# Values as scaled float16 pairs, two product passes, and one DMA transpose per half of p

## The chip, the cores and the metric

The kernel runs on one core of a Trainium2 chip. Five engines matter: PE multiplies matrices, DVE, ACT and POOL work on vectors, and SP issues DMAs from one queue in program order. Each engine takes its instructions strictly in the order in which the program holds them; semaphores make one wait for another. The metric is the device time of one execution in microseconds (us), lower is better.

## The reference

Eight batches of eight heads of attention with 576 tokens and head size 64, masked by blocks of 64, followed by a two-layer network on all 4608 tokens. Everything is float32.

```python
scores = (1 / np.sqrt(64)) * np.matmul(q, k.transpose(0, 1, 3, 2))
scores = np.where(pos[:, None] // 64 >= pos[None, :] // 64, scores, -1e9)
scores = scores - np.max(scores, axis=-1, keepdims=True)
attn = np.exp(scores)
attn = attn / (np.sum(attn, axis=-1, keepdims=True) + 1e-09)
x = np.matmul(attn, v)             # then (B, H, S, D) -> (B*S, H*D) = (4608, 512)
h = x @ w_in                       # (512, 2048)
out = np.maximum(0.01 * h, h) @ w_out   # (2048, 512)
```

## The kernel before

**Order of the work.** The body of the kernel does not run instructions, it records them. `add(choices, rank, reads, writes, ...)` stores one operation with the engines that could do it, a rank and the keys of the buffers that it reads and writes. `Plan.run` then plays the program with a small table of costs (for SP, `TISSUE` and `TTILE` say what it believes the issue of a DMA transpose to cost) and writes out a fixed order for each engine: whichever operation is ready in that play and has the lowest rank goes next. The constants `RL`, `RV`, `RX`, `RN`, `LEAD`, `LAG` and so on shift the ranks, in units of one head. On the chip the order is fixed; only the waits are real.

**Heads.** `attention(i)` records one head. The eight heads of the first batch are done in two parts ("lo", "hi") by plain float32 products while the weights of the network are loaded and split. The other 56 heads (8 to 63, kind "full") are what the change is about. Such a head has its scores on PE, its maxima on DVE, exponentials on ACT (tiles `prow` or `slab`, five tiles t = 0 to 4 of up to 128 query rows), and its row sums in `sums`, inverted into `rec`.

**p in halves.** `parting(t)` multiplies the exponentials by `rec` into a float16 high half `part(0)`, and takes the float16 rest as low half `part(1)`. The tile holds both halves interleaved in blocks of 128 columns. `turn` issues one DMA transpose per tile on SP that moves both halves into `turned[y2]`: five per head, of 2, 4, 6, 8 and 10 blocks. `turned` has two buffers, y2 = 0 and 1, used by every other head. So a head's first transpose waits for PE to have finished the product of the head two before.

**v in three terms.** The values come by one DMA per head; `vs` keeps them as three bfloat16 terms v0, v1, v2 (two copies and two subtractions on ACT, DVE or POOL). In the product, `inner(j, y, w)` multiplies the weights [v0|v1] with both halves of p and the weights [v2|0] with the high half: three passes over 512, 448, 320 and 192 columns. `outer(w)` does the pieces for the first and the last 64 tokens as two products of 256 and 128 columns into another PSUM bank, whose partial sums DVE adds up by a `tensor_reduce` over three column groups (L760) and two additions (L769). `put_x` adds the upper 64 rows of the PSUM tile to the lower ones (L256/L255, L715) and stores x.

**The network.** `scale_x` takes the sum of squares of finished tokens on ACT and a scale from it; `split_x` makes float16 pairs of x; `ffn1` and `ffn2` are the two layers in chunks of 256 tokens, three passes each, with their results in `p_h` and `p_o`. They are recorded with ranks between the heads' and fill PE between the heads. When attention is over the rest of them remains.

**SP's queue** holds, per full head, the load of q and k (L495), the load of v (L505), five transposes (L633), and now and then stores of the output (L897).

Of the kernel before, what the change touches and what calls it, by code (L numbers as in the profile page):

```python
# [35 lines left out]
DB0 = 16  # L36

RL = 2.512
RP = 0.116
RB = 0.594  # L40
RT = 2.547
RV = 2.777
RX = -0.691
RN = -0.668

LEAD = 3.0
LAG = 1.993
RS = 2.157
RG = -0.11
OFF1 = 4.036  # L50
OFF2 = -1.346
SL1 = 11.386
AHEAD = -0.758

LAT = 1550
HOLD = 262.256
# [182 lines left out]
def attention_ffn(ctx: ExitStack, tc: tile.TileContext, qk0: bass.AP, qk: bass.AP, v: bass.AP, w_in: bass.AP, w_out: bass.AP, out: bass.AP):  # L239
# [62 lines left out]
    vs = fixed([P, NT, 2, 2 * D], BF16, "vs", 2)  # L302
# [3 lines left out]
    for y in range(2):  # L306
        nc.gpsimd.memset(sums[y], 1.0)
        nc.gpsimd.memset(nm[y], 0.0)
        nc.gpsimd.memset(vs[y][:, :, 1, D : 2 * D], 0.0)
    xr = [fixed([P, ND, S], F32, "xr0"), None]  # L310
    raws = fixed([P, 2 * WIDE], I32, "raw", RAWS)
# [4 lines left out]
    diag = fixed([P, P], F32, "diag")  # L316
    both = fixed([P, 1], F32, "both")
    p_s = fixed([P, 2, 512], F32, "p_s", pool=psum)
# [11 lines left out]
    ob = [fixed([P, DM], F32, "ob"), None]  # L330

# [15 lines left out]
    parts = [[carve(y, [t + 1, 2, P], F16) for t in range(NT)] for y in range(2)]  # L347
    v_stage = [carve(y, [NT, D], F32) for y in range(2)]
# [14 lines left out]
    def weight_piece(num, rank, f, out_side):  # L363
# [98 lines left out]
    def attention(i):  # L462
# [38 lines left out]
        if plain_v:  # L501
            vt, vkey = lambda: vf[z][:, :nv], ("vf", z)
        else:
            vt, vkey = lambda: v_stage[y2][:, :nv], ("vt", y2)
        add([("SP", 475, lambda: nc.sync.dma_start(vt(), v[b, h, :, :nv]))], r0 - RL + VD, [], [vkey], lag=1.5 * dma(nv * P * D * 4))  # L505
# [14 lines left out]
        if not plain_v:  # L520
            v0, v1, v2 = vs[z][:, :, 0, 0:D], vs[z][:, :, 0, D : 2 * D], vs[z][:, :, 1, 0:D]
# [86 lines left out]
        def parting(t):  # L608
            n, c = qn[t], pc[t]
            by = rec[z][:n, t : t + 1]  # L610

            def p():
                x = rows_[t][:n, c:]
                return x if t == 0 else x.rearrange("p (j k) -> p j k", k=P)

            def part(y):
                x = parts[y2][t][:n]
                return x[:, 0, y, c:] if t == 0 else x[:, :, y, :]

            w = pw[t] - c  # L620
            add([
                ("POOL", pool1(w), lambda: nc.gpsimd.tensor_scalar(part(0), p(), by, 1.0, op0=ALU.mult, op1=ALU.mult)),
                ("ACT", act(w, True), lambda: nc.scalar.mul(part(0), p(), by)),  # L623
                ("DVE+", dve(w, True), lambda: nc.vector.tensor_scalar_mul(part(0), p(), by)),
            ], r0 - RN, [("rec", z, t)] + pkeys(t), [("ph", y2, t)])
            add([
                ("DVE+", dve(w), lambda: nc.vector.scalar_tensor_tensor(part(1), p(), by, part(0), op0=ALU.mult, op1=ALU.subtract)),  # L627
            ], r0 - RN, [("rec", z, t), ("ph", y2, t)] + pkeys(t), [("pl", y2, t)])

            def turn():  # L630
                src = parts[y2][t][:n].rearrange("p j y k -> p (j y k)")
                dst = turned[y2][:, 8:10, 2, BLK:P] if t == 0 else turned[y2][:, 0 : 2 * t + 2, t - 1, :]
                nc.sync.dma_start_transpose(dst, src)  # L633
# [59 lines left out]
        ptd = [("ptf", g[0]) for g in tgroups[kind]] if plain_v else [("pt", y2, t) for t in range(NT)]  # L693
# [14 lines left out]
        def put_x(x, c, t0, t1):  # L708
            n, dst, keys = t1 - t0, place(t0, t1), keys_of(t0, t1)
            if plain_v:  # L710
                add(copying(n, dst, lambda: p_t[x][0:64, c : c + n], sb=False), rx, [("t", x)], keys)
                return
            add(copying(n, dst, lambda: p_t[x][64:128, c : c + n], sb=False), rx, [("t", x)], keys)
            add(
                [("DVE", dve(n), lambda: nc.vector.tensor_add(dst(), p_t[x][0:64, c : c + n], dst()))],  # L715
# [23 lines left out]
        def inner(j, y, w):  # L739
            c = 128 * j - 64 if j else 0  # L740
            start, stop = j == 0 and y == 0 and w == 0, j == 3 and w == 1

            def go():
                src = turned[y2][:, 2 * j + y].rearrange("p t k -> p (t k)")[:, c:512]
                nc.tensor.matmul(p_t[x1][:, c:512], vs[z][:, j + 1, w, :], src, start=start, stop=stop)  # L745
# [3 lines left out]
        def outer(w):  # L749
            def go():  # L750
                src = turned[y2][:, 8 : 10 - w, 2:4, BLK:P]
                dst = p_t[x0][:, 2 * w * P : (2 + w) * P].rearrange("p (c a b) -> p c a b", a=2, b=BLK)
                nc.tensor.matmul(dst, vs[z][:, 0, w, :], src, start=True, stop=True)

            return RATEH * (2 - w) * P, go, LOADH
# [3 lines left out]
        add(  # L759
            [("DVE", dve(6 * BLK), lambda: nc.vector.tensor_reduce(  # L760
                p_t[x0][:, 6 * BLK : 8 * BLK], p_t[x0][:, : 6 * BLK].rearrange("p (c k) -> p k c", c=3), axis=AX.X, op=ALU.add
            ))], rx, [], [("t", x0)],
        )
        put_x(x0, 6 * BLK, 0, 64)
        put_x(x1, 0, *tokens[kind])
        late = place(512, 576)
        for r in (0, 64):
            add(
                [("DVE", dve(64), lambda r=r: nc.vector.tensor_add(late(), p_t[x0][r : r + 64, 7 * BLK : 8 * BLK], late()))],  # L769
                rx, [("t", x0)], keys_of(512, 576),  # L770
            )
# [34 lines left out]

    def regions(c0, c1):
# [8 lines left out]
    def scale_x(e, c0, c1, rank):  # L816
        spans_ = list(regions(c0, c1))
        for k, (_, b, o, ln, keys) in enumerate(spans_):

            def square(k=k, b=b, o=o, ln=ln):  # L820
                nc.scalar.activation(
                    junk[:, :, :ln], xr[b % 2][:, :, o : o + ln], AF.Square, accum_out=xn[:, 2 * e + k : 2 * e + k + 1]
                )

            add([("ACT", act(4 * ln, True) + 190, square)], rank, keys, [("xn", e, k), "junk"])
        x = bank()
        num = len(spans_)

        def total(k):
            nc.tensor.matmul(p_t[x][:, 0:1], ones, xn[:, 2 * e + k : 2 * e + k + 1], start=k == 0, stop=k == num - 1)  # L830
# [90 lines left out]
    for i in range(len(work) + 1):  # L921
        if i == 2 * H:

            def second(y):
                nc.gpsimd.memset(parts[y][0], 0.0)
                if y:
                    clear(prow[1])

            for y in range(2):
                new = [("ph", y, 0), ("vt", y)] + [(a, y, t) for t in range(NT) for a in ("ph", "pl", "pt")]  # L930
                new += [("p", 1, t) for t in range(NT)] + [(a, 1, d) for a in ("xh", "xl") for d in range(0, CH, BLK)] if y else [("x", 1, h, k) for h in range(H) for k in (0, 1)] + [("ob", 1)]
                kind = "wo" if y else "wi"
                add([("POOL", 1500 if y else 200, lambda y=y: second(y))], 0, [("val", bool(y), f) for f in range(NF)], new)
        if i in events:
# [5 lines left out]
            for k in range(num):  # L940
# [5 lines left out]
                ffn2(c, e, u, rank + (nxt - i) * LAG / num + 0.003)  # L946
        if i < len(work):
# [42 lines left out]
```

## Time and profile before

| | |
|---|---|
| median of 3 runs | 1123.3 us (1120.63 to 1124.39) |
| the profiled execution's own time | 1120.48 us |
| its span in the trace | 1118.7 us |
| busy: PE, DVE, ACT, POOL | 1070.5, 747.9, 670.8, 322.8 us |
| granted PE clock over the span | 0.988 |
| DMA transposes | 280, 3.2 us from issue to landing (median) |

The profile comes from one execution; times inside it count from the span's start. The execution's time is 1.8 us longer than the span. SP has no busy row of its own on the page, since issuing DMAs is not counted as busy; its instructions stand in the timeline as "SPq". A row of the timeline merges instructions of one kind that follow each other: start, length of the whole stretch, what, and how many (x10). In the view of a line, "min/median/max" are the lengths of single instructions.

### The profile page before, as it was taken

The numbers are of one execution on the slowest core, as the hardware profiler recorded it, in microseconds if no ns is written. First come the engines' busy times: TensorE is split into PE (matmuls) and PEld (weight loads), VectorE is DVE, ScalarE is ACT, GpSimd is POOL, SyncE is SP. The second block draws the span as 40 slices with busy tenths as digits, with TensorE's granted clock in tenths as the row PEclk, the third lists the DMA queues.
The fourth block names the chain that finished last, engine by engine and source line by source line (L and its number), as shares of the span: only waits on it lengthen the run. The fifth ranks groups of instructions, "written<-read, shape, count | busy, mean of one in ns | idle before, by whom it ended". The sixth has DMA issues, their size and how long they took to land.

```text
span 1118.7 us, 20505 instructions
## 1 busy us (share of the span) xinstructions
PE 1070.5 (96%) x7298; PEld 745.8 (67%) x7298; DVE 747.9 (67%) x1814; ACT 670.8 (60%) x1650; POOL 322.8 (29%) x339
## 2 busy tenths in 40 slices
PE   9999899858999999999999999999999999999998
PEld 7887566535666666666666666666667666666665
DVE  6888978888877877786766667787777777220000
ACT  6797767657666666664455656666666666332222
POOL 2114324434433233323232223322333232111221
PEclk9999999978999999999999999999999999999999
DMA  7747247675755556564636355665555544100000
GB/s 260 248 145 262 81 97 174 132 170 123 165 140 122 128 123 142 123 123 106 116 83 117 80 127 121 141 129 105 122 141 138 114 101 93 27 20 1 20 19 19
DMA packets 247461, 131.37 MB, mean 117 GB/s; under 512 B 220224, under 2 KB 229440, under 8 KB 247360
## 3 DMA queue, kind: packets, MB, share of 16 engines
q1 hardware_dynamic: 247360, 130.07, 49.2%
q8 instruction: 57, 0.93, 0.3%
q14 instruction: 44, 0.36, 0.1%
HBM read 67.37 MB, written 9.44 MB: 69 GB/s over the span
## 4 chain that ended last, share of the span: by engine, by line
PE 37%; DVE 25%; ACT 6%; issue 4%; DVEq 0%; ACTq 0%
PE p_o L885 16%; PE p_h L867 16%; DVE nm L564 6%; DVE slab L627 5%; PE p_t L745 3%; PE p_s L544 2%; ACT prow L581 2%; DVE qs L514 2%; ACT slab L581 1%; DVE p_t L760 1%; ACT slab L623 1%; DVE slab L265 1%; DVE vs L265 1%; DVE slab L715 1%; DVE kk L256 1%
## 5 line engine op out<-in xcount | busy, mean ns | idle before, releaser
L266 POOL TENSOR_TENSOR gl<-g,gh 128x512 bf16<-128x512 f32 x121 | 144.2, 1192 | 475.8 <-ACT gh L255 431.4
L867 PEld LDWEIGHTS <-wih 128*128 128x128 f16 x2304 | 224.2, 98 | 77.2 <-issue 1.1
L867 PE MATMUL p_h<-slab,wih 128*128 128x256 f16 x1152 | 196.8, 273 | 0.0
L564 DVE TENSOR_REDUCE nm<-p_s 128x1 f32<-128x320 f32 (+4 forms) x308 | 143.6, 489 | 44.8 <-ACT prow L581 23.1
L885 PE MATMUL p_o<-woh,gh 128*128 128x512 f16 x576 | 172.6, 381 | 0.0
L885 PE MATMUL p_o<-wol,gh 128*128 128x512 f16 x576 | 172.3, 381 | 0.0
L885 PE MATMUL p_o<-woh,gl 128*128 128x512 f16 x576 | 172.3, 381 | 0.0
L872 ACT ACTIVATE g<-p_h 128x512 f32<-128x512 f32 x144 | 85.2, 592 | 139.5 <-PE p_h L867 139.2
L885 PEld LDWEIGHTS <-gh 128*128 128x128 f16 x1152 | 108.2, 99 | 82.9 <-issue 1.2
L867 PE MATMUL p_h<-slab,wil 128*128 128x256 f16 x576 | 157.2, 273 | 0.0
L867 PE MATMUL p_h<-xh,wih 128*128 128x256 f16 x576 | 157.1, 273 | 0.0
L867 PE MATMUL p_h<-xl,wih 128*128 128x256 f16 x576 | 157.0, 273 | 0.0
L867 PE MATMUL p_h<-xh,wil 128*128 128x256 f16 x576 | 157.0, 273 | 0.0
L544 PE MATMUL p_s<-kk,qs 128*128 128x288 f32 (+2 forms) x592 | 122.8, 334 | 33.6 <-ACT prow L581 22.3
L581 ACT ACTIVATE prow<-p_s,nm 128x320 f32<-128x320 f32 (+4 forms) x168 | 88.9, 531 | 87.0 <-DVE nm L564 82.9
L581 ACT ACTIVATE slab<-p_s,nm 128x448 f32<-128x448 f32 (+4 forms) x140 | 73.2, 524 | 88.7 <-DVE nm L564 87.9
L867 PEld LDWEIGHTS <-wil 128*128 128x128 f16 x1152 | 112.8, 98 | 13.2
L544 PEld LDWEIGHTS p_s<-kk,qs 128*128 128x128 f32 x592 | 91.1, 193 | 44.7 <-ACT prow L581 26.6
L745 PE MATMUL p_t<-slab,vs 128*128 128x512 f16 (+3 forms) x672 | 118.9, 328 | 0.0
L885 PEld LDWEIGHTS <-gl 128*128 128x128 bf16 x576 | 56.6, 98 | 68.6 <-issue 1.1
L745 PEld LDWEIGHTS <-vs 128*128 128x128 bf16 x672 | 64.3, 100 | 45.5 <-issue 4.5
L627 DVE SCALAR_TENSOR_TENSOR slab<-prow,rec,slab 128x512 f16<-128x512 f32 (+4 forms) x140 | 83.9, 643 | 13.2 <-ACT slab L623 13.2
(126 smaller groups left out, 1502.1 us busy)
## 6 DMA issues: line engine op xcount, KB each, us to landing
qk_in<-in_qk SPq DMA_DIRECT2D x56, 576.0 KB, 4.0
slab<-in_v SPq DMA_DIRECT2D x56, 160.0 KB, 3.2
raw<-in_w_in SPq DMA_DIRECT2D x16, 512.0 KB, 4.8
raw<-in_w_out SPq DMA_DIRECT2D x16, 512.0 KB, 4.2
out<-ob SPq DMA_DIRECT2D x18, 256.0 KB, 2.1
out<-slab SPq DMA_DIRECT2D x18, 256.0 KB, 2.4
slab<-slab SPq DMA_TRANSPOSE x280, 3.2
qk_in<-in_qk SPq DMA_DIRECT2D x8, 416.0 KB, 4.2
```

The lines of the kernel that those rows point to most:

```text
L256: two = lambda: nc.vector.tensor_copy(dst(), src())
L265: ("DVE+" if sb else "DVE", dve(n), lambda: nc.vector.tensor_sub(dst(), one(), two())),
L266: ("POOL", pool2(n), lambda: nc.gpsimd.tensor_sub(dst(), one(), two())),
L514: [("DVE+", dve(qe - qa), lambda: nc.vector.scalar_tensor_tensor(qd[64:128], q_in[64:128], scale, qd[64:128], op0=ALU.mult, op1=ALU.subtra ...
L544: go = lambda ap=ap, cols=cols, c=c, k0=k0, k1=k1, first=first, last=last: nc.tensor.matmul(ap, qs[z][:, cols], kk[z][:, c, k0:k1], start= ...
L564: [("DVE", dve(kw[t]), lambda t=t, ap=ap, flat=flat: nc.vector.tensor_reduce(nm[z][: qn[t], t : t + 1], ap[: qn[t]], axis=AX.X if flat els ...
L581: nc.scalar.activation(o, ap[: qn[t]], AF.Exp, bias=nm[z][: qn[t], t : t + 1], scale=scale / 2 if plain_s else 1.0, accum_out=sums[z][: qn ...
L627: ("DVE+", dve(w), lambda: nc.vector.scalar_tensor_tensor(part(1), p(), by, part(0), op0=ALU.mult, op1=ALU.subtract)),
L745: nc.tensor.matmul(p_t[x1][:, c:512], vs[z][:, j + 1, w, :], src, start=start, stop=stop)
L867: nc.tensor.matmul(hh[:, i, :], w[:, f, d, :], x[:, d, :], start=k == 0, stop=k == len(terms) - 1)
L872: add([("ACT", act(512), lambda: nc.scalar.activation(g[z], hh, AF.Prelu, alpha=0.01, scale=DOWN))], rank, [("h", z)], [("g", z)])
L885: nc.tensor.matmul(p_o[m], a[:, i, m * P : (m + 1) * P], w[:, 2 * u + i, :], start=u == 0 and k == 0, stop=u == NU - 1 and k == 5,)
```

## The change

The change has these parts:

- v is loaded for four heads at once into `v_raw` (`v_group`, GROUP = 4): 14 DMAs in place of 56. ACT takes the sum of squares of the group, one small product with ones on PE adds it over the partitions, and three small DVE operations make from it a power of two `vsc` and its inverse `vin`.
- `vs` holds two float16 terms of the scaled values: one scaling (ACT, POOL or DVE) and one scale-and-subtract (DVE or POOL) per head. The products have two passes, [v0|v1] against the high and the low half of p. `put_x` multiplies by `vin` on the way out.
- The outer pieces are four products of 64 columns; two of them accumulate into the bank of the inner products, so the reduction L760 and the additions L769 are gone.
- The two halves of p lie one after the other in `parts`, without the padding blocks being rewritten (64 columns fewer for each of the four wide tiles), and each half has a DMA transpose of its own: ten per head, of 1 to 5 blocks.
- `scale_x` takes its squares by halves of the heads, `diag` and `junk` share or shrink buffers, and all rank constants and the play's costs (`TISSUE` 500 to 250, `HOLD`) are refitted, so the order of nearly everything shifts somewhat.

SP's order, the piece that holds the transposes of two heads early in the stretch of full heads (`slab_74` and `slab_75` are the buffers of even and odd heads; the last numbers are the shape written: partitions, blocks, columns). Before:

```order
L495 DMA qk_in_89<-in_qk 128x1152
L633 DMA_TRANSPOSE slab_74<-slab_74 128x8x128
L633 DMA_TRANSPOSE slab_74<-slab_74 128x2x64
L633 DMA_TRANSPOSE slab_74<-slab_74 128x4x128
L633 DMA_TRANSPOSE slab_74<-slab_74 128x6x128
L633 DMA_TRANSPOSE slab_74<-slab_74 128x10x128
L633 DMA_TRANSPOSE slab_75<-slab_75 128x8x128
L633 DMA_TRANSPOSE slab_75<-slab_75 128x2x64
L633 DMA_TRANSPOSE slab_75<-slab_75 128x4x128
L633 DMA_TRANSPOSE slab_75<-slab_75 128x6x128
L633 DMA_TRANSPOSE slab_75<-slab_75 128x10x128
```

The same place in the changed program:

```order
L649 DMA_TRANSPOSE slab_74<-slab_74 128x4x128 x2
L649 DMA_TRANSPOSE slab_74<-slab_74 128x1x64 x2
L649 DMA_TRANSPOSE slab_74<-slab_74 128x2x128 x2
L649 DMA_TRANSPOSE slab_74<-slab_74 128x3x128 x2
L649 DMA_TRANSPOSE slab_74<-slab_74 128x5x128 x2
L649 DMA_TRANSPOSE slab_75<-slab_75 128x4x128 x2
L649 DMA_TRANSPOSE slab_75<-slab_75 128x1x64 x2
L649 DMA_TRANSPOSE slab_75<-slab_75 128x2x128 x2
L649 DMA_TRANSPOSE slab_75<-slab_75 128x3x128 x2
L649 DMA_TRANSPOSE slab_75<-slab_75 128x5x128 x2
L502 DMA qk_in_90<-in_qk 128x1152
```

Each transpose has become two of half as many blocks; SP has ten in a row per head. Later in the program the load of q and k of the head three further on, and the stores, still stand between two heads' transposes, and none of the 56 loads of v does, except one group load every fourth head.

PE's order at the end of one head's product with the values. Before:

```order
L745 LDWEIGHTS vs_96
L745 MATMUL p_t_123<-slab_75,vs_96 128x192
L745 LDWEIGHTS vs_96
L745 MATMUL p_t_123<-slab_75,vs_96 128x192
L745 LDWEIGHTS vs_96
L745 MATMUL p_t_123<-slab_75,vs_96 128x192
L753 LDWEIGHTS vs_96
L753 MATMUL p_t_124<-slab_75,vs_96 128x256
L753 LDWEIGHTS vs_96
L753 MATMUL p_t_124<-slab_75,vs_96 128x128
L544 MATMUL p_s<-kk_93,qs_91 128x448
```

And in the changed program:

```order
L765 LDWEIGHTS vs_95
L765 MATMUL p_t_129<-slab_74,vs_95 128x320
L771 LDWEIGHTS vs_95
L771 MATMUL p_t_129<-slab_74,vs_95 128x64
L771 LDWEIGHTS vs_95
L771 MATMUL p_t_129<-slab_74,vs_95 128x64
L765 LDWEIGHTS vs_95
L765 MATMUL p_t_129<-slab_74,vs_95 128x192
L765 LDWEIGHTS vs_95
L765 MATMUL p_t_129<-slab_74,vs_95 128x192
L563 MATMUL p_s<-kk_94,qs_92 128x288 x4
```

Each width now comes twice instead of three times, and two of the products of 64 columns stand among the inner ones, in the same bank. The product of head h stands behind the scores of head h + 2 in both programs.

The core of the diff:

```diff
@@ attention: v
+            e = (i - 2 * H) // GROUP
+            k = (i - 2 * H) % GROUP
+            vkey, by, back = ("vr", e % 2, k), vsc[:, e : e + 1], vin[:, e : e + 1]
+            vt = v_raw[e % 2][:, k].rearrange("p (t d) -> p t d", d=D)
+            v0, v1 = vs[z][:, :, 0:D], vs[z][:, :, D : 2 * D]
...
-            add(copying(nv * D, lambda: v0, vt), rp, [vkey], [("vs", z)])
-            add(subtracting(nv * D, vt, vt, lambda: v0, "POOL"), rp, [("vs", z)], [vkey])
-            add(copying(nv * D, lambda: v1, vt), rp, [vkey], [("vs", z)])
-            add(subtracting(nv * D, lambda: v2, vt, lambda: v1, "POOL"), rp, [vkey], [("vs", z)])
+            add([
+                ("ACT", act(nv * D, True), lambda: nc.scalar.mul(v0, vt, by)),
...
+            ], r0 - RW, [vkey, ("vsc", e)], [("vs", z)])
+            add([
+                ("DVE+", dve(nv * D), lambda: nc.vector.scalar_tensor_tensor(v1, vt, by, v0, op0=ALU.mult, op1=ALU.subtract)),
+                ("POOL", pool1(nv * D) + pool2(nv * D), twice),
+            ], r0 - RW, [("vsc", e)], [("vs", z), vkey])
@@ parting
-            def turn():
-                src = parts[y2][t][:n].rearrange("p j y k -> p (j y k)")
-                dst = turned[y2][:, 8:10, 2, BLK:P] if t == 0 else turned[y2][:, 0 : 2 * t + 2, t - 1, :]
-                nc.sync.dma_start_transpose(dst, src)
-
-            tiles = (t + 1) * 2 * n // 16
-            add([("SP", TISSUE + TTILE * tiles, turn)], r0 - RN, [("ph", y2, t), ("pl", y2, t)], [("pt", y2, t)], lag=1000 * TMOVE * (t + 1) * n / P)
+            for y in range(2):
+
+                def turn(y=y):
+                    dst = turned[y2][:, 8 + y : 9 + y, 2, BLK:P] if t == 0 else turned[y2][:, y : 2 * t + 2 : 2, t - 1, :]
+                    nc.sync.dma_start_transpose(dst, parts[y2][t][:n, y])
+
+                tiles = (t + 1) * n // 16
+                add([("SP", TISSUE + TTILE * tiles, turn)], r0 - RN, [("ph", y2, t, y)], [("pt", y2, t, y)], lag=500 * TMOVE * (t + 1) * n / P)
@@ the product
-        add([("PE", [outer(0), outer(1)])], rv, [("pt", y2, 0), ("pt", y2, 4), vkey], [("t", x0)])
-        add([("PE", [inner(j, y, w) for j in range(4) for y, w in ((0, 0), (1, 0), (0, 1))])], rv, ptd + [vkey], [("t", x1)])
-        add(
-            [("DVE", dve(6 * BLK), lambda: nc.vector.tensor_reduce(
...
+        add([("PE", [outer(x0, 0, 2, y, y == 0, y == 1) for y in range(2)])], rv, [("pt", y2, 0, y) for y in range(2)] + [vkey], [("t", x0)])
+        turns_ = [inner(j, y) for j in range(3) for y in range(2)] + [outer(x1, 448, 3, y, False, False) for y in range(2)]
+        add([("PE", turns_ + [inner(3, y) for y in range(2)])], rv, ptd + [vkey], [("t", x1)])
@@ new
+    def v_group(e):
+        i0 = 2 * H + GROUP * e
...
+        add([("SP", 475, lambda: nc.sync.dma_start(buf, v[b, h : h + GROUP].rearrange("h p t d -> p h (t d)")))], rank, [], keys + first, lag=1.5 * dma(GROUP * NT * P * D * 4))
+        add([("ACT", act(GROUP * NT * D, True) + 190, lambda: nc.scalar.activation(junk, flat, AF.Square, accum_out=vn[:, one]))], rank, keys, [("vn", e), "junk"])
+        add([("PE", [(60, lambda: nc.tensor.matmul(p_t[x][:, 0:1], ones, vn[:, one], start=True, stop=True))])], rank, [("vn", e)], [("t", x)])
```

More of the change, by code (lines that the diff above doesn't have):

```diff
@@ L36 @@
 DB0 = 16
[L38 to L46, printed above, removed]
-LAG = 1.993
[L48 to L53, printed above, removed]
+GROUP = 4
+AHEADV = 3
+RW = 0.824
+RL = 3.087
+RP = -0.207
+RB = 0.485
+RT = 2.64
+RV = 2.523
+RX = -1.556
+RN = -0.648
+LEAD = 2.936
+LAG = 1.993
+RS = 2.645
+RG = -0.127
+OFF1 = 4.292
+OFF2 = -1.368
+SL1 = 10.904
+AHEAD = 0.017
 LAT = 1550
-HOLD = 262.256
+HOLD = 238.695
 FILL = 235
@@ L301, in attention_ffn @@
     kk = fixed([P, 2, S], F32R, "kk", 2)
-    vs = fixed([P, NT, 2, 2 * D], BF16, "vs", 2)
+    vs = fixed([P, NT, 2 * D], F16, "vs", 2)
     nm = fixed([P, NT], F32, "nm", 2)
@@ L308, in attention_ffn @@
         nc.gpsimd.memset(nm[y], 0.0)
-        nc.gpsimd.memset(vs[y][:, :, 1, D : 2 * D], 0.0)
     xr = [fixed([P, ND, S], F32, "xr0"), None]
-    raws = fixed([P, 2 * WIDE], I32, "raw", RAWS)
+    raw = fixed([P, RAWS, 2 * WIDE], I32, "raw")
+    raws = [raw[:, k] for k in range(RAWS)]
+    v_raw = [fixed([P, GROUP, NT * D], F32, "v_raw"), raw.rearrange("p a b -> p (a b)")[:, : GROUP * NT * D].bitcast(F32).rearrange("p (h n) -> p h n", h=GROUP)]
+    junk = fixed([P, GROUP * NT * D], BF16, "junk")
     ptf = fixed([P, 1024], F32, "ptf")
@@ L315, in attention_ffn @@
     we = fixed([P, 2], I32, "we")
-    diag = fixed([P, P], F32, "diag")
     both = fixed([P, 1], F32, "both")
+    xn, xs, xi = (fixed([P, n], F32, m) for n, m in ((40, "xn"), (10, "xs"), (10, "xi")))
+    vn, vsc, vin = (fixed([P, 14], F32, m) for m in ("vn", "vsc", "vin"))
+    xe, ve = fixed([P, 10], I32, "xe"), fixed([P, 14], I32, "ve")
     p_s = fixed([P, 2, 512], F32, "p_s", pool=psum)
@@ L346, in attention_ffn @@
     turned = [carve(y, [2 * NT, NT - 1, P], F16) for y in range(2)]
-    parts = [[carve(y, [t + 1, 2, P], F16) for t in range(NT)] for y in range(2)]
-    v_stage = [carve(y, [NT, D], F32) for y in range(2)]
+    parts = [[carve(y, [2, pw[t]], F16) for t in range(NT)] for y in range(2)]
     xr[1] = carve(0, [ND, S], F32)
@@ L610, in parting @@
             by = rec[z][:n, t : t + 1]
-            def p():
-                x = rows_[t][:n, c:]
-                return x if t == 0 else x.rearrange("p (j k) -> p j k", k=P)
+            w = kw[t]
+            p = rows_[t][:n, c : c + w]
             def part(y):
-                x = parts[y2][t][:n]
-                return x[:, 0, y, c:] if t == 0 else x[:, :, y, :]
-            w = pw[t] - c
+                return parts[y2][t][:n, y, c : c + w]
             add([
[L622 to L625, printed above, removed]
+                ("POOL", pool1(w), lambda: nc.gpsimd.tensor_scalar(part(0), p, by, 1.0, op0=ALU.mult, op1=ALU.mult)),
+                ("ACT", act(w, True), lambda: nc.scalar.mul(part(0), p, by)),
+                ("DVE+", dve(w, True), lambda: nc.vector.tensor_scalar_mul(part(0), p, by)),
+            ], r0 - RN, [("rec", z, t)] + pkeys(t), [("ph", y2, t, 0)])
@@ L712, in put_x @@
                 return
-            add(copying(n, dst, lambda: p_t[x][64:128, c : c + n], sb=False), rx, [("t", x)], keys)
-            add(
-                [("DVE", dve(n), lambda: nc.vector.tensor_add(dst(), p_t[x][0:64, c : c + n], dst()))],
+            add([
+                ("ACT", act(n) + 93, lambda: nc.scalar.mul(dst(), p_t[x][64:128, c : c + n], back[64:128])),
+                ("DVE", dve(n), lambda: nc.vector.tensor_scalar_mul(dst(), p_t[x][64:128, c : c + n], back[64:128])),
+            ], rx, [("t", x)], keys)
+            add(
+                [("DVE", dve(n), lambda: nc.vector.scalar_tensor_tensor(
+                    dst(), p_t[x][0:64, c : c + n], back[0:64], dst(), op0=ALU.mult, op1=ALU.add
+                ))],
                 rx, [("t", x)], keys,
@@ L737, in attention, with inner @@
             return
-        def inner(j, y, w):
+        def inner(j, y):
             c = 128 * j - 64 if j else 0
-            start, stop = j == 0 and y == 0 and w == 0, j == 3 and w == 1
             def go():
                 src = turned[y2][:, 2 * j + y].rearrange("p t k -> p (t k)")[:, c:512]
-                nc.tensor.matmul(p_t[x1][:, c:512], vs[z][:, j + 1, w, :], src, start=start, stop=stop)
+                nc.tensor.matmul(p_t[x1][:, c:512], vs[z][:, j + 1], src, start=j == 0 and y == 0, stop=j == 3 and y == 1)
@@ L747, in inner, with outer @@
             return RATEH * (512 - c), go, LOADH
-        def outer(w):
+        def outer(x, c, tt, y, start, stop):
             def go():
[L751 to L755, printed above, removed]
-        add([("PE", [outer(0), outer(1)])], rv, [("pt", y2, 0), ("pt", y2, 4), vkey], [("t", x0)])
@@ L758, in attention @@
-        add([("PE", [inner(j, y, w) for j in range(4) for y, w in ((0, 0), (1, 0), (0, 1))])], rv, ptd + [vkey], [("t", x1)])
-        add(
[L760 to L764, printed above, removed]
-        put_x(x1, 0, *tokens[kind])
[L766 to L771, printed above, removed]
+                nc.tensor.matmul(p_t[x][:, c : c + BLK], vs[z][:, 0], turned[y2][:, 8 + y, tt, BLK:P], start=start, stop=stop)
@@ L805, in attention_ffn @@
     tokens = {"full": (64, 576), "lo": (0, 320), "hi": (320, 576)}
+    def v_group(e):
+        i0 = 2 * H + GROUP * e
+        b, h = divmod(work[i0][0], H)
+        buf = v_raw[e % 2]
+        rank, keys = i0 - RL + VD - 1, [("vr", e % 2, k) for k in range(GROUP)]
+        first = [("raw", k) for k in range(RAWS)] if e == 1 else []
+        add([("SP", 475, lambda: nc.sync.dma_start(buf, v[b, h : h + GROUP].rearrange("h p t d -> p h (t d)")))], rank, [], keys + first, lag=1.5 * dma(GROUP * NT * P * D * 4))
+        one = slice(e, e + 1)
+        flat = buf.rearrange("p h n -> p (h n)")
+        add([("ACT", act(GROUP * NT * D, True) + 190, lambda: nc.scalar.activation(junk, flat, AF.Square, accum_out=vn[:, one]))], rank, keys, [("vn", e), "junk"])
+        x = bank()
+        add([("PE", [(60, lambda: nc.tensor.matmul(p_t[x][:, 0:1], ones, vn[:, one], start=True, stop=True))])], rank, [("vn", e)], [("t", x)])
+        add([("DVE", 68, lambda: halved(ve[:, one], p_t[x][:, 0:1]))], rank, [("t", x)], [("ve", e)])
+        first, second = powers(lambda: ve[:, one], lambda: vsc[:, one], lambda: vin[:, one])
+        add([("DVE+", 68, first)], rank, [("ve", e)], [("vsc", e)])
+        add([("DVE+", 68, second)], rank, [("ve", e)], [("vin", e)])
     def regions(c0, c1):
@@ L818, in scale_x, with square @@
         for k, (_, b, o, ln, keys) in enumerate(spans_):
[L820 to L825, printed above, removed]
+            for y in range(2):
+                def square(k=2 * k + y, b=b, o=o, ln=ln, y=y):
+                    nc.scalar.activation(
+                        junk[:, : 2 * ln].rearrange("p (a b) -> p a b", a=2), xr[b % 2][:, 2 * y : 2 * y + 2, o : o + ln],
+                        AF.Square, accum_out=xn[:, 4 * e + k : 4 * e + k + 1],
+                    )
+                near = [x for x in keys if x[2] // 4 == y]
+                add([("ACT", act(2 * ln, True) + 190, square)], rank, near, [("xn", e, 2 * k + y), "junk"])
         x = bank()
-        num = len(spans_)
+        num = 2 * len(spans_)
         def total(k):
-            nc.tensor.matmul(p_t[x][:, 0:1], ones, xn[:, 2 * e + k : 2 * e + k + 1], start=k == 0, stop=k == num - 1)
+            nc.tensor.matmul(p_t[x][:, 0:1], ones, xn[:, 4 * e + k : 4 * e + k + 1], start=k == 0, stop=k == num - 1)
         one = slice(e, e + 1)
@@ L946, in attention_ffn @@
                 ffn2(c, e, u, rank + (nxt - i) * LAG / num + 0.003)
+        if (i + AHEADV) >= 2 * H and (i + AHEADV) % GROUP == 0 and i + AHEADV < len(work):
+            v_group((i + AHEADV - 2 * H) // GROUP)
         if i < len(work):
```

39 lines of the change are left out of this document (20 added, 19 removed).

## The prediction

> **What bounds the kernel now.** I read the page's busy rows first, then the busy times by stretch, then SP's timeline.
>
> ```profile
> PE 1070.5 (96%) x7298; PEld 745.8 (67%) x7298; DVE 747.9 (67%) x1814; ACT 670.8 (60%) x1650; POOL 322.8 (29%) x339
> core 0: us, PE busy (x) PEld busy (x) DVE busy (x) ACT busy (x) POOL busy (x), PEclk, DMA share, GB/s
> 160.00:200.00 40.00, 35.30 (x231) 23.23 (x228) 33.40 (x80) 27.22 (x72) 16.84 (x15) 1.00 0.73 154
> 200.00:240.00 40.00, 29.88 (x176) 19.36 (x176) 34.10 (x84) 28.78 (x80) 16.52 (x19) 0.91 0.75 156
> 240.00:280.00 40.00, 29.19 (x166) 20.15 (x167) 34.13 (x86) 25.93 (x65) 15.45 (x16) 0.83 0.58 129
> 440.00:480.00 40.00, 40.00 (x279) 27.91 (x278) 30.35 (x75) 27.87 (x71) 13.34 (x12) 1.00 0.61 135
> 560.00:600.00 40.00, 40.00 (x280) 28.00 (x279) 24.06 (x59) 20.08 (x49) 11.95 (x13) 1.00 0.43 86
> 1000.00:1040.00 40.00, 40.00 (x281) 27.24 (x280) 2.64 (x3) 9.89 (x17) 8.08 (x7) 1.00 0.04 14
> ```
>
> There are three stages. Up to about 280 us PE is not full and DVE is the fullest engine. From 280 us on PE is full in nearly every stretch, first with heads and network mixed, then, once attention is over, with the network alone. So PE's work counts from 280 us on, as long as nothing holds it up. What could hold it up is SP, which feeds the products:
>
> ```profile
> 432.46 7.91 SPq L633 DMA_TRANSPOSE slab<-slab  x5
> 440.47 0.53 SPq L495 DMA_DIRECT2D qk_in<-in_qk  x1
> 441.09 0.38 SPq L897 DMA_DIRECT2D out<-ob  x1
> 441.52 0.42 SPq L505 DMA_DIRECT2D slab<-in_v  x1
> 446.52 8.25 SPq L633 DMA_TRANSPOSE slab<-slab  x5
> 460.56 8.21 SPq L633 DMA_TRANSPOSE slab<-slab  x5
> SPq L633 <- PE p_t L745: 102.4, 43, 4.2
> ```
>
> A head comes every 14.05 us (432.46, 446.52, 460.56), and about 5 us of that SP has nothing to issue. The last row, of SP's waits, says what it waits for: in 43 heads the first transpose waits for PE to finish the product that read the same buffer. SP has slack today, PE has none.
>
> **PE: what goes.** The product of one head:
>
> ```profile
> 444.28 0.34 PE L753 MATMUL p_t<-slab,vs 128*128 128x256 f16 x2
> 444.45 2.03 PE L745 MATMUL p_t<-slab,vs 128*128 128x512 f16 x12
> 446.32 0.59 PE L885 MATMUL p_o<-woh,gh 128*128 128x512 f16 x2
> 508.38 1.87 PE p_t L745 x12
> 643.34 1.87 PE p_t L745 x12
> 971.69 1.87 PE p_t L745 x12
> L830 PE MATMUL p_t<-xn,ones 128*128 128x1 f32 x30 | 4.2, 232 | 2.0 <-DVE slab L769 1.1 <-ACT junk L821 1.0
> ```
>
> The twelve inner products run from 444.45 to the start of the next at 446.32, 1.87 us for three passes (the three rows of the chain of waits say the same of heads 33, 40 and 63). Two passes take 1.25 us: 0.62 us less per head, 34.7 us over 56 heads. The outer ones took 444.28 to 444.45, 0.17 us for 384 columns. Four of 64 columns cost between 0.11 us (by columns) and 0.23 us (if each costs what one of 128 does, 0.17 / 3 = 0.057); I take 0.17, no change. New are 14 sums of values and 15 more of tokens on PE: the 15 sums of today are 30 records and 4.2 us, so 29 cost 8.1 us; with the wait in front of them (2.0 / 15 each) it would be 12 us, below it nothing where PE waits anyway. I take nothing, for the reason given next. **If PE set the pace throughout, a head would come every 14.05 - 0.62 = 13.43 us.**
>
> **SP: what is added.** This is the step on which I decide. Ten transposes must be issued per head in place of five.
>
> ```profile
> L633 SPq DMA_TRANSPOSE slab<-slab x280: 1157/1242/2337, 154.9 to 954.2; - x140
> 181.99 1.38 SPq L633 DMA_TRANSPOSE slab<-slab  x1
> 185.02 1.16 SPq L633 DMA_TRANSPOSE slab<-slab  x1
> 154.88 1.34 SPq L633 DMA_TRANSPOSE slab<-slab  x1
> 156.94 13.17 SPq L633 DMA_TRANSPOSE slab<-slab  x9
> 176.72 14.15 SPq L633 DMA_TRANSPOSE slab<-slab  x10
> 193.38 8.98 SPq L633 DMA_TRANSPOSE slab<-slab  x5
> 205.13 8.20 SPq L633 DMA_TRANSPOSE slab<-slab  x5
> slab<-slab SPq DMA_TRANSPOSE x280, 3.2
> ```
>
> The issue of one takes 1157 ns at least and 1242 in the median, over shapes from 2 to 10 blocks. The two single rows are, by SP's order, one of 10 blocks (181.99) and one of 2 (185.02): five times the data, 0.22 us more. So the price is mostly per instruction, and half a transpose costs nearly a whole one. What ten in a row take, this trace shows itself: at 176.72 the transposes of two heads stand behind each other, 14.15 us; nine at 156.94 took 13.17. From below, ten medians with the gap of 0.05 that the shortest neighbours leave are 12.9 us, ten minima 12.1. From above, the row of nine gives 14.6. Halves save about 0.03 us each (0.22 us for 8 blocks, and a half has 3 fewer on average, less whatever of the 0.22 is scatter). I take 1.34 us each, between median and the row of ten: 13.4 us. Beside them stand the load of q and k (0.53), a quarter of a load of v (0.42 / 4), 26 stores of 0.38 that SP's order has among the 56 heads (0.18 per head), and a gap for each: 0.9 us. **SP needs S = 14.3 us per head, with bounds of 13.0 and 15.5, and PE only 13.43.** SP becomes the bound. PE then waits 0.9 us in each head, and in these waits its new small sums are hidden.
>
> [...]
>
> **Vector engines: what goes.**
>
> ```profile
> L760 DVE TENSOR_REDUCE p_t<-p_t 128x128 f32<-128x384 f32 x56 | 30.1, 538 | 17.3 <-PE p_t L753 16.9
> L769 DVE TENSOR_TENSOR slab<-p_t,slab 64x64 f32<-64x64 f32 x64 | 14.2, 222 | 2.0
> L769 DVE TENSOR_TENSOR xr<-p_t,xr 64x64 f32<-64x64 f32 x48 | 10.6, 221 | 1.5
> L265 DVE TENSOR_TENSOR slab<-slab,vs 128x320 f32<-128x320 f32 x36 | 17.4, 485 | 0.6
> L265 DVE TENSOR_TENSOR vs<-slab,vs 128x320 bf16<-128x320 f32 x34 | 16.9, 497 | 1.7 <-ACT vs L255 0.8
> L255 ACT CAST vs<-slab 128x320 bf16<-128x320 f32 x100 | 45.3, 453 | 23.7 <-DVE slab L265 15.1 <-POOL slab L266 8.0
> ```
>
> DVE loses 30.1 + 24.8 + 34.3 us, gains at most 56 scale-and-subtracts of about 0.49 us (27), and saves a little on 64 columns per wide tile: some 60 to 80 us, over 1 us per head. ACT loses 45.3 and gains 56 scalings of 0.45 (25) and 14 squares of 1280 columns: about even. From 280 us on this is worth nothing, for PE was the bound there. Before 280 us DVE set a pace of 11.7 us per head (193.38 to 205.13) and would now allow about 10.5; but SP's 14.3 is longer than both. There the change loses outright: what is late next is the product, and behind it on PE the network's work in the fixed order.
>
> **The sum**, against the execution of 1120.5 us (span 1118.7 plus 1.8; the median of the runs is 1123.3, so this execution is one of the faster). I leave the first transpose at 154.9. Heads 8 and 9: 20 x 1.34 = 26.8, to 181.7; landing 3.2 and product 1.25 give 186.2, when head 10 may start, since it takes the buffer of head 8. Heads 10 to 33 at 14.3 each: 343.2, and 4.45 for landing and product, 533.9 (before: head 33 ended at 508.38 + 1.87 = 510.2). Then come eight heads between which the changed order holds a bigger share of the network; PE needs 19.28 us there today ((643.34 - 508.38) / 7), so 18.66 now, which is over S: 149.3, to 683.2. SP has caught up by then, and head 43 starts with the end of head 41's product. Heads 43 to 63, 21 x 14.3 = 300.3, and 4.45: 987.9 (before: 973.6). PE's work behind the last product is the network alone, the same in both orders: 1118.7 - 973.6 = 145.1. With the 1.8: **1134.8 us, call it 1135**. In short 491.3 + 45 S; S = 13.98 would break even. PE's gain of 0.62 us per head is thus eaten by 0.9 us of waiting per head, and by about 3 us per head up to 280 us.
>
> **Rivals.**
>
> (a) Issue goes by data. If half a transpose takes half the time, ten take what five take (7.91 to 8.25 us), SP keeps its slack, and PE is the bound: 1120.5 - 34.7 + 8.1 for the new sums = 1094, less what a lighter DVE gives back before 280 us (about ten heads at 1.2 us): 1082. Against it stand 1157 ns for the smallest.
>
> (b) SP binds at the cheap end. With S = 13.0 (ten minima) SP sets the pace only up to head 33, 186.2 + 312 + 4.45 + 149.3, and then PE with 22 x 13.43 = 295.5: 1094; with S = 13.7 it is 1111, and at 13.98 nothing is won. For it speak the many rows of 1.23 us; against it the longer ones, up to 2337 ns, which come in long rows too (the ten in 14.15 us cannot be without them).
>
> (c) SP at its dear end: with the row of nine as price S = 15.5 and the sum 1189. The same holds if the stores, which wait for the network's results, block the transposes behind them. Against it: with SP late, what it waits for is done when its turn comes.
>
> (d) The change does not do what it says on PE: if products of 64 columns cost far more than 0.057 us each. It would be hidden in PE's waits, and the time that of the forecast.
>
> **How the numbers follow.** The forecast, with S from 14.0 to 14.9 (1120 to 1162), has a chance of 0.62; (a) 0.13; (b) 0.15, of which 0.03 lies next to no change; (c) 0.10. (d) changes none of them. About 0.3% is what a measurement of this kernel tells from no change. Faster: (a), 0.12 of (b), 0.01 of the forecast, 0.26; the same: 0.03 of (b) and 0.02 of the forecast, 0.05; slower: the rest, 0.69. The range leaves out (a) and most of (c): 1090 to 1165; the forecast's own is 1120 to 1162.
>
> **What would show it.** Right: SP's timeline from 155 us on has rows of ten and more transposes with next to no gap, 1.3 to 1.4 us each; the pace up to 280 us is near 14 us per head; PE shows waits in front of the product, ended by the landing of a transpose, and its busy share falls in the stretches from 280 to 500 us; the same 145 us follow the last product. Wrong: transposes near 0.7 us, SP still waiting for PE in most heads, and PE full from 280 us on.

## The result, and the profile after

The changed kernel takes 1165.9 us (median of 4 runs, 1163.32 to 1167.37) against 1122.97 us for the kernel before: a ratio of 1.0382, 95% interval 1.0356 to 1.0408. It is slower, as forecast, but by 43 us where 14 were forecast, and it lies 0.9 us above the stated range. The profiled execution took 1165.96 us, its span is 1164.2.

The page of the changed kernel, the busy row, and the busy times by stretch (the columns are those of the view shown before):

```profile
PE 1064.4 (91%) x7264; PEld 742.7 (64%) x7264; DVE 681.8 (59%) x1707; ACT 676.2 (58%) x1583; POOL 330.0 (28%) x345
200.00:240.00 40.00, 29.34 (x172) 19.17 (x173) 23.49 (x52) 21.99 (x53) 11.67 (x13) 0.87 0.53 114
240.00:280.00 40.00, 18.60 (x75) 10.76 (x73) 24.00 (x63) 20.81 (x55) 10.05 (x14) 0.71 0.58 114
440.00:480.00 40.00, 31.07 (x200) 20.71 (x200) 20.21 (x52) 20.65 (x51) 9.36 (x9) 0.87 0.49 112
560.00:600.00 40.00, 36.25 (x239) 24.80 (x238) 19.32 (x49) 20.78 (x47) 12.78 (x13) 0.91 0.53 105
840.00:880.00 40.00, 28.73 (x192) 19.77 (x190) 21.27 (x58) 21.94 (x55) 10.52 (x10) 0.83 0.53 123
1040.00:1080.00 40.00, 40.00 (x278) 27.05 (x277) 2.64 (x3) 9.51 (x17) 7.45 (x7) 1.00 0.04 14
```

PE's busy time has hardly fallen although a third of the passes of the values' product is gone; in the stretches up to 280 us DVE, the fullest engine before with 34 of 40 us, is down to 24. Nothing is full there. Later there are stretches in which PE has 9 to 11 us of idle time (440, 840). PE's busy sum also holds products at a lower granted clock: in these rows the clock is low where PE idles (0.71 with 18.60 of 40 us busy, 0.87 with 31.07, 1.00 with 40.00), and over the span it is 0.957 against 0.988.

SP's timeline and the view of the line that issues the transposes:

```profile
159.12 26.71 SPq L649 DMA_TRANSPOSE slab<-slab  x20
189.07 26.92 SPq L649 DMA_TRANSPOSE slab<-slab  x20
216.09 0.52 SPq L502 DMA_DIRECT2D qk_in<-in_qk  x1
216.71 14.13 SPq L649 DMA_TRANSPOSE slab<-slab  x10
230.90 0.57 SPq L502 DMA_DIRECT2D qk_in<-in_qk  x1
...
527.25 12.88 SPq L649 DMA_TRANSPOSE slab<-slab  x10
...
572.02 16.67 SPq L649 DMA_TRANSPOSE slab<-slab  x10
588.74 0.58 SPq L502 DMA_DIRECT2D qk_in<-in_qk  x1
593.25 13.78 SPq L649 DMA_TRANSPOSE slab<-slab  x10
...
706.47 14.10 SPq L649 DMA_TRANSPOSE slab<-slab  x10
...
1002.83 13.41 SPq L649 DMA_TRANSPOSE slab<-slab  x10
L649 SPq DMA_TRANSPOSE slab<-slab x560: 1102/1218/2784, 159.1 to 1015.0; - x187
```

SP now issues with next to no pause, but for waits of 2 to 6 us for PE in front of heads 37 to 43 (the first of them ends at 593.25). The half transposes take 1218 ns in the median, the whole ones took 1242: half the data saves 24 ns. From head 10 (189.07) to head 33 (527.25) a head comes every 338.18 / 23 = 14.70 us, from head 43 (706.47) to head 63 (1002.83) every 14.82 us. The last head's transposes end at 1016.24.

Some other waits were not there before. From the view of waits, ACT's and PE's; then ACT's timeline around one of them, SP's for the same time, and PE's:

```profile
ACT junk L824 <- DMA v_raw<-in_v: 48.7, 5, 14.0
PE p_s L563 <- ACT slab L600: 25.3, 7, 11.3
PE p_s L563 <- ACT prow L600: 16.8, 7, 7.7
PE p_t L771 <- DMA slab<-slab: 20.9, 15, 5.3
PE p_t L765 <- DMA slab<-slab: 19.9, 12, 4.3
456.04 1.27 ACT L824 ACTIVATE junk<-v_raw 128x1280 bf16<-128x1280 f32 x1 [11.47 <-DMA v_raw<-in_v]
459.83 0.63 ACT L600 ACTIVATE slab<-p_s,nm 128x448 f32<-128x448 f32 x1
435.56 14.34 SPq L649 DMA_TRANSPOSE slab<-slab  x10
450.00 0.52 SPq L502 DMA_DIRECT2D qk_in<-in_qk  x1
450.57 0.43 SPq L821 DMA_DIRECT2D v_raw<-in_v  x1
462.18 0.61 PE L563 MATMUL p_s<-kk,qs 128*128 128x288 f32 x1 [8.93 <-ACT slab L600]
```

The last two rows of waits, 41 us together, are the forecast wait of the product for the transposes (p_t is its PSUM tile). The first three rows hold a wait that was not forecast. The load of a group of v is issued at 450.57, behind the ten transposes that SP began at 435.56, and lands some 5.5 us later. ACT stood in front of its sum of squares for 11.47 us; the exponentials of the next scores (459.83) stood behind it in ACT's order, and PE, which needs the PSUM of these scores free, was idle for 8.93 us up to 462.18. There are four such places (355, 462, 582 and 853 us), all at a group that is the first of a batch; PE's four idle stretches add up to 7.7 + 8.9 + 3.7 + 11.3 = 31.6 us. ACT's fifth wait for v (4.4 us, at 727 us) was followed by no such stretch.

### The profile page after: what moved, and what is told of

It reads as the page before. It is cut to its first block, busy times and chain, and to the rows that moved or that the text cites. A ratio compares the mean times of both kernels' runs of the same rounds, so it can differ in the third digit from the quotient of the medians.

```text
span 1164.2 us, 20758 instructions
## 1 busy us (share of the span) xinstructions
PE 1064.4 (91%) x7264; PEld 742.7 (64%) x7264; DVE 681.8 (59%) x1707; ACT 676.2 (58%) x1583; POOL 330.0 (28%) x345
## 5 line engine op out<-in xcount | busy, mean ns | idle before, releaser
L269 POOL TENSOR_TENSOR gl<-g,gh 128x512 bf16<-128x512 f32 x132 | 155.2, 1176 | 390.2 <-ACT gh L258 339.9
L914 PE MATMUL p_o<-woh,gh 128*128 128x512 f16 x576 | 175.5, 387 | 0.0
L563 PE MATMUL p_s<-kk,qs 128*128 128x288 f32 (+2 forms) x592 | 128.9, 346 | 42.2 <-ACT slab L600 25.3
L563 PEld LDWEIGHTS p_s<-kk,qs 128*128 128x128 f32 x592 | 96.1, 201 | 54.9 <-ACT slab L600 29.0
L765 PE MATMUL p_t<-slab,vs 128*128 128x512 f16 x448 | 94.1, 348 | 19.9 <-DMA slab<-slab 19.9
L643 DVE SCALAR_TENSOR_TENSOR slab<-prow,rec,slab 128x448 f16<-128x448 f32 (+4 forms) x140 | 79.6, 606 | 48.3 <-ACT slab L639 43.3
L269 POOL TENSOR_TENSOR kk<-qk_in,kk 128x576 fp32r<-128x576 f32 x51 | 74.8, 1466 | 80.5 <-DVE kk L259 49.4
```

What stands on the lines that cost most here:

```text
L269: ("POOL", pool2(n), lambda: nc.gpsimd.tensor_sub(dst(), one(), two())),
L563: go = lambda ap=ap, cols=cols, c=c, k0=k0, k1=k1, first=first, last=last: nc.tensor.matmul(ap, qs[z][:, cols], kk[z][:, c, k0:k1], start= ...
L765: nc.tensor.matmul(p_t[x1][:, c:512], vs[z][:, j + 1], src, start=j == 0 and y == 0, stop=j == 3 and y == 1)
L914: nc.tensor.matmul(p_o[m], a[:, i, m * P : (m + 1) * P], w[:, 2 * u + i, :], start=u == 0 and k == 0, stop=u == NU - 1 and k == 5,)
```

## The experiments

Theory S: issuing a transpose costs about the same whatever its size (1.22 us in the median for the halves, 1.24 for the whole ones); ten per head keep SP busy all the time, SP sets the pace of the heads, and late loads of v behind them block ACT. Its rivals: the group load of v or the new order are the main loss (V, O, R), or the transposes' data (rival (a) of the prediction).

### One transpose per tile

```diff
-            for y in range(2):
-                def turn(y=y):
-                    ... one half of parts[y2][t] -> every other block of turned
+            def turn():
+                src = parts[y2][t][:n].rearrange("p j y k -> p (j y k)")   # both halves, as before
+                nc.sync.dma_start_transpose(dst, src)
```

(The interleaved layout of the halves and the padding come back with it, and the price that the play uses for an issue is that of the kernel before.)

> The changed kernel with one part undone: one DMA transpose per tile of p (five per head, both halves interleaved as before), everything else as changed. Theory S (issuing costs about 1.3 us per transpose whatever its size, so ten per head saturate SP, and late loads of v behind them block ACT): SP needs some 7.5 us per head again, waits for PE in most heads, PE is full from 280 us on, 1085 to 1097 us. Rival R (the refitted constants and the new order, or the group load of v, make the time): SP slack comes back but the time stays above 1123 us.

Measured: 1093.49 us (4 runs), ratio to the kernel before 0.9757, interval 0.9736 to 0.9777. Faster than both kernels. SP's timeline, PE's product of one head, and one stretch of the busy times there:

```profile
416.95 8.04 SPq L652 DMA_TRANSPOSE slab<-slab  x5
430.34 8.07 SPq L652 DMA_TRANSPOSE slab<-slab  x5
443.86 8.19 SPq L652 DMA_TRANSPOSE slab<-slab  x5
457.23 3.29 SPq L652 DMA_TRANSPOSE slab<-slab  x2
402.00 0.23 PE L774 MATMUL p_t<-slab,vs 128*128 128x64 f16 x2
402.06 1.25 PE L768 MATMUL p_t<-slab,vs 128*128 128x512 f16 x6
403.14 0.22 PE L774 MATMUL p_t<-slab,vs 128*128 128x64 f16 x2
403.20 0.33 PE L768 MATMUL p_t<-slab,vs 128*128 128x192 f16 x2
403.37 0.59 PE L917 MATMUL p_o<-woh,gh 128*128 128x512 f16 x2
440.00:480.00 40.00, 40.00 (x291) 28.42 (x290) 30.32 (x78) 28.18 (x64) 14.69 (x13) 1.00 0.65 160
```

A head comes every (457.23 - 416.95) / 3 = 13.43 us, PE's own need, PE is full (40.00 of 40 us), and SP has 4 to 5 us of slack again. The product runs from 402.00 to 403.37, 1.37 us where it was 2.04 (444.28 to 446.32). All other parts of the change but those named above are in this kernel, ACT's long waits for v are gone, and it is faster: the split of the transposes is the part that costs, and rival R falls.

### The kernel before, with the transposes split

```diff
-            def turn():   # 5 per head, both halves
+            for y in range(2):
+                def turn(y=y):   # 10 per head, one half each
```

(The code is shortened here. The halves then lie one after the other, as in the changed kernel, and the play's price of an issue is that of the changed kernel too, so the order shifts with it. Nothing else of the change is in.)

> The kernel before with one part of the change alone: each tile's transpose split into one for the high and one for the low half, ten per head; values still in three terms, one load of v per head. Theory S: ten issues of 1.37 us and 1.3 us of loads and stores are about 15.1 us per head against PE's 14.05 (19.3 between heads 33 and 41): 1160 to 1180 us, with no waits of ACT for v. Rival R: the split alone costs little, 1123 to 1135 us.

Measured: 1167.09 us, ratio 1.0416 (1.0382 to 1.045). SP's timeline in the stage that PE filled before:

```profile
435.20 14.58 SPq L633 DMA_TRANSPOSE slab<-slab  x10
449.87 0.53 SPq L495 DMA_DIRECT2D qk_in<-in_qk  x1
450.45 0.42 SPq L505 DMA_DIRECT2D slab<-in_v  x1
450.98 14.18 SPq L633 DMA_TRANSPOSE slab<-slab  x10
```

The split makes the loss without the rest of the change, with three passes and one load of v per head. ACT waits for v here too, other than expected, but only four times, 1.6 to 5.7 us, and all before 240 us. The kernel is as slow as the changed one although PE has a third pass to do: SP sets the pace (15.0 us per head from head 10 to 33 and again from 43 to 63), and the passes do not count.

### Nine transposes

```diff
+            if t == 0:
+
+                def both_():   # the halves of the smallest tile together
+                    nc.sync.dma_start_transpose(turned[y2][:, 8:10, 2, BLK:P], parts[y2][0][:n].rearrange("p y k -> p (y k)"))
+
+                add([("SP", TISSUE + TTILE * n // 8, both_)], r0 - RN, ...)   # "..." left out
+                return
```

> The changed kernel with the two halves of the smallest tile (t = 0) moved by one transpose: nine per head in place of ten, the same bytes. Theory S: SP needs 14.7 - 1.37 = 13.35 us per head, just under PE's 13.43; 24 heads save 1.37 us each up to head 33, and behind head 41 PE sets the pace: about 1105 to 1118 us. If issue went by data (rival a of the prediction) nothing would change: 1160 to 1168 us.

Measured: 1117.49 us (8 runs), ratio 0.9963 (0.9947 to 0.9979). SP's timeline at heads 43 and 63:

```profile
674.76 11.42 SPq L656 DMA_TRANSPOSE slab<-slab  x8
948.99 10.33 SPq L656 DMA_TRANSPOSE slab<-slab  x8
```

A head comes every (948.99 - 674.76) / 20 = 13.71 us there, and every 13.53 us from head 10 to 33, where it was 14.82 and 14.70. One issue fewer per head, with the same bytes, is worth 48 us by the medians. The bytes are the same, so a price by data would have given nothing; rival (a) falls. Between ten (1165.9), nine (1117.5) and five (1093.5) the gain per issue is 48 us, then 6: from head 43 on nine need about what PE needs (13.71 us per head, with five 13.65), and most of the 24 us that are left between nine and five lie between heads 10 and 33, where five take 12.64 us per head.

### The loads of q and k from ACT's queue

```diff
-                nc.sync.dma_start(qkt, qk[b - 1, h])
+                (nc.scalar if kind == "full" else nc.sync).dma_start(qkt, qk[b - 1, h])
...
-        add([("SP", 475, load)], r0 - RL, [], [qkey], lag=1.3 * dma((nq + ke) * rows * 4))
+        add([("ACT" if kind == "full" else "SP", 475, load)], r0 - RL, [], [qkey], lag=1.3 * dma((nq + ke) * rows * 4))
```

> The changed kernel with the load of q and k of each full head issued from ACT's DMA queue in place of SP's; the ten transposes stay. Theory S: SP's need per head falls by the 0.57 us of that load, 14.7 to 14.1; in 45 heads SP sets the pace, 26 us: 1132 to 1148 us. If it is not SP's issue time that counts (but, say, how long transposes take to land), nothing changes: 1160 to 1170 us.

Measured: 1142.31 us, ratio 1.0199 (1.0172 to 1.0226), 24 us less than the changed kernel by the medians, 20 by the ratios. SP's row there shows what is left:

```profile
439.57 42.89 SPq L649 DMA_TRANSPOSE slab<-slab  x30
```

30 transposes, those of three heads, without a break, 1.43 us each. The transposes are untouched and land 2.6 us after their issue in the median, as in the changed kernel, and yet a head comes every 14.06 us from head 10 to 33 and every 14.22 us from head 43 to 63, about 0.6 us less than before this edit. So it is SP's issue time that counts, here that of a plain load. ACT's waits for v are shorter too (22 us in all against 48.7), so not all of the gain need be the pace.

### The group load of v earlier

```diff
-        add([("SP", 475, lambda: nc.sync.dma_start(buf, v[...]))], rank, ...)
+        add([("SP", 475, lambda: nc.sync.dma_start(buf, v[...]))], rank - 1, ...)   # and AHEADV 3 -> 4; "..." left out
```

> The changed kernel with only the group load of v placed one head earlier in SP's order. Theory S, second part: ACT's four waits of 8 to 14 us for the load of v vanish, and with them PE's four idle stretches of 4 to 11 us (32 us in all). SP keeps its pace of 14.7 us per head, and most of PE's idle time was slack beside it: 1148 to 1160 us. Rival V (the late load of v, not the number of transposes, is the main loss): the whole 32 us come back and the time is near 1134 us or under it.

Measured: 1169.97 us, ratio 1.0431 (1.0409 to 1.0453): neither time that was expected. The waits did not go away, and SP's timeline shows why:

```profile
ACT junk L824 <- DMA v_raw<-in_v: 45.6, 5, 13.7
442.59 14.07 SPq L649 DMA_TRANSPOSE slab<-slab  x10
456.76 0.52 SPq L502 DMA_DIRECT2D qk_in<-in_qk  x1
457.32 0.43 SPq L821 DMA_DIRECT2D v_raw<-in_v  x1
```

The load stands where it stood in the changed kernel, behind the same ten transposes and the same load of q and k. Only three of the 14 group loads moved, to 40, 80 and 120 transposes after the first in place of 50, 90 and 128; from the sixth group on every load stands behind as many transposes as before (160, 200, 240 and so on), though its rank is lower. So the edit did not do what was meant for four of the five groups for which ACT waits; for the other one (at 349 us in the changed kernel) the wait fell from 8.0 to 6.0 us. What holds the loads there was not tried; a group's load overwrites the buffer of the group two before, and may have to wait for that in the play. The run tells nothing about the two theories; its first transposes start 3.3 us later (162.4 against 159.1), which is about the 4 us that it lost.

### The sum of squares later on ACT

```diff
+    def v_scale(e):   # the sum and what follows it, out of v_group; recorded just ahead of head i0
...
-        add([...], rank, keys, [("vn", e), "junk"])
+        add([...], rank, keys + ([("p", (i0 - 2) % 2, 4)] if i0 > 2 * H else []), [("vn", e), "junk"])
```

> The changed kernel; the load of v stays where it is, but ACT's sum of squares of the group is placed behind the exponentials of the head two before the group, about two heads later in ACT's order (the run with the earlier load had moved this sum along with the load, so ACT still waited 8 to 14 us). Theory S: SP keeps its 14.7 us per head; ACT's long waits for v and PE's idle stretches of 4 to 11 us before scores are gone; only what of them was not slack beside SP comes back, some 12 to 16 us: 1147 to 1158 us. Rival V (the late load of v is the main loss): 1123 to 1136 us.

(The remark on the run with the earlier load does not hold: there neither the loads nor the sums moved from the sixth group on. Here the loads stay, and the sums of the groups for which ACT waited stand one to two heads later in ACT's order.)

Measured: 1155.49 us, ratio 1.0315 (1.0295 to 1.0335). The waits of PE's scores, and the transposes of heads 33 and 43 in SP's timeline:

```profile
PE p_s L563 <- ACT prow L600: 10.9, 13, 2.4
PE p_s L563 <- ACT slab L600: 6.8, 11, 1.4
529.25 13.40 SPq L649 DMA_TRANSPOSE slab<-slab  x10
698.13 13.87 SPq L649 DMA_TRANSPOSE slab<-slab  x10
```

ACT no longer waits for v (it now waits 16 times for q and k, 4.2 us at most), and of PE's idle stretches in front of scores none is longer than 2.4 us. That is worth 10 us by the medians and 7.5 us by the ratios, out of 31.6 us of idle time. Nearly all of it lies between heads 33 and 43: 698.13 - 529.25 = 168.9 us, where the changed kernel took 706.47 - 527.25 = 179.2. Elsewhere SP's pace (14.62 us per head from head 10 to 33 here, 14.74 from 43 to 63) hides the rest. Rival V falls as the main loss; the late load is a smaller part that comes with SP's delay.

### The order made with the measured price

```diff
-TISSUE, TTILE, TMOVE = 250, 25, 0.25
+TISSUE, TTILE, TMOVE = 1260, 1.3, 0.25
```

> The changed kernel with the table from which the order is made told what the issue of a transpose costs here (1260 ns and 1.3 ns per tile of 16 by 128, in place of 250 and 25 per tile); the instructions are the same, their order is not. Theory S: SP still needs 14.7 us per head up to head 33 and behind head 41, where PE's share per head in the new order is 13.4 to 14.7: 1140 to 1158 us, the long waits for v gone. Rival O (the fixed order, made with a price too low, is the main loss, and ten transposes can be hidden): 1095 to 1123 us.

Measured: 1142.08 us (6 runs), ratio 1.0207 (1.0189 to 1.0226). The same instructions in an order that knows the price lose 24 us less by the medians, 20 by the ratios. Most of it lies between heads 33 and 43, which take 161.0 us (519.40 to 680.36) in place of 179.2; part of that is the waits for v. SP's pace is hardly another (14.51 and 14.67 us per head). The other half of the loss stays, so rival O is at most half right: neither of the two orders that were run with ten issues and nothing else changed hides them. (For a half transpose of average size, 23.2 tiles, the new table says 1290 ns; the 560 issues of the changed kernel's trace took 1283 ns on average.)

### One transpose per tile, order with the measured price

```diff
 (the first experiment)
-TISSUE, TTILE, TMOVE = 500, 25, 0.25
+TISSUE, TTILE, TMOVE = 1260, 1.3, 0.25
```

> One transpose per tile in the changed kernel, as in the run with five per head (1093.5 us), with the order made with the measured price of an issue. SP has slack with five per head, so the order should matter little: 1085 to 1098 us by every theory; below 1085 would say that the order still cost something there.

Measured: 1093.39 us, ratio 0.9757 (0.9738 to 0.9777), the same as with the old price. With SP off the path its price in the order does not matter. These two kernels are the fastest of the study.

## Why the prediction was right and wrong

**The bound.** Right. PE's share of the product fell as worked out (0.67 us per head, 0.62 predicted, 13.43 us per head when PE sets the pace, exactly as worked out), and SP took its place.

**The price of half a transpose.** Right in kind: 1218 ns against 1242 in the median. Half the data saves 24 ns, so nearly all of the price was paid per instruction, as the prediction read it from one transpose of 10 blocks and one of 2 (1.38 and 1.16 us).

**The term that was too small: SP's need per head.** The prediction put S at 14.3 us between bounds of 13.0 and 15.5; the trace gives 14.70 and 14.82. Both parts of it were too small. The transposes were priced at 1.34 us each, 13.4 per head; heads whose ten stand in one piece take 13.7 us on average (12.87 to 16.67), 1.37 each, because about one in 15 is long (up to 2784 ns). The trace before had it too: its 280 issues take 1.32 us on average, where the median is 1.24, and a gap, 0.09 us in the median, comes on top. The loads, stores and gaps beside them were put at 0.9 us and take 1.0 to 1.1. Every 0.1 us of S is worth 4.5 us by the prediction's own formula, 491.3 + 45 S; with 14.70 it gives 1153, close to the 1155.5 of the run in which ACT does not wait for v.

**The step that was missing: the load of v behind the transposes.** The change's new chain (load of v, sum on ACT, sum on PE) was costed only on PE, as small sums "hidden" in PE's waits. That the load stands in SP's queue behind ten transposes, that ACT waits for it in order, and that the exponentials stand behind ACT's wait was not followed up; the prediction names what waits for SP as the product alone, and so put this wait at nothing. By the run with the later sum it cost 7.5 to 10 us. It is this that carried the time past the prediction's upper end; S as measured lay within its bounds.

**By stretches.** The 31 us between forecast and trace can be followed by the starts of the heads' transposes. Head 10 starts at 189.07 (186.2 predicted): 2.9 us, because the first transposes came at 159.12 where 154.9 was carried over from the trace before. From head 10 to 33 it is 338.2 us against 23 x 14.3 = 328.9: 9.3 us, by S. From head 33 to 43 the prediction's terms make 168.1 us (515.1 to 683.2), which the run with the later sum has (168.9) and the changed kernel has not (179.2): 11.1 us, by ACT's wait at 577 us. There PE was idle for only 3.7 us, but the transposes of head 36 took 16.67 us and the next head began 21.2 us after it (572.02 to 593.25); how the rest of the 11 us comes about was not taken apart. From there on PE set the pace as predicted, 18.6 us per head. From head 43 to 63 it is 20 times 14.82 against 14.3: 10.4 us, by S. At the end 2.6 us come back: the last transposes end at 1016.24, the product 2.7 us later, and 145.2 us follow (145.1 predicted).

**The rivals.** (a) fell with the run of nine. (b) did not come: S was above its middle, not below. (c) had the right sign for the error but not its size; the stores did not block the transposes: from 189 us to the last transpose SP's longest wait for a store's data was 0.9 us (at 702 us), and there it waited for PE right after. (d) fell: in the run with one transpose per tile two products of 64 columns start 0.06 us before the next one (402.00 to 402.06). The bound of 1165 was drawn with most of (c) left out and no room for a wait other than SP's own, and was too low by a little. That the time came so near to it is luck: the bound stood for an S near 15, and what carried the time there was an S of 14.7 to 14.8 together with the wait of ACT.

**Open.** The long issues (1.7 to 2.8 us) come about once in 15 transposes, before (18 of 280) and after (38 of 560). What makes them was not tried. Why the first transposes came 4.2 us later was not tried either.

## What to carry to other kernels

Count DMA instructions, not only bytes: an issue had a nearly fixed price here (1.22 us in the median for half a transpose, 1.24 for a whole one), and splitting each transpose in two took the queue from some 8 us per head to 13.7. Before splitting, compare the queue's need per step with the step's pace, from a row in which it issues without a break, and take the mean of such a row, with its outliers, not the median. When a queue becomes late, look at everything that stands in it, and at which engine waits in order for each of these: one load behind ten transposes stopped ACT (11.47 us), and ACT stopped PE (8.93 us).

## What the runs showed of the hardware

The issue of a DMA transpose took 1.10 us at least and 1.22 us in the median for 1 to 5 blocks of 128 columns, 1.16 and 1.24 us for 2 to 10 blocks, where the load of q and k, 576 KB in one DMA, took 0.53 us in the median behind transposes (0.33 us before the first of them). Half transposes landed 2.6 us after their issue in the median, whole ones after 3.2. In both traces PE's products (7298 before, 7264 after), the instructions of DVE (1814, 1707), ACT (1649, 1582) and POOL (339, 345) and SP's DMAs (492, 730) stand in the order of the program.
